# Weight chunks loaded early into idle buffers, and some counts moved to ScalarE, in a top-k attention and SoLU kernel

## The chip, the cores and the metric

The kernel runs on one core of a Trainium2 chip. The metric is the device time of one execution in microseconds (us). Engines are called by the names of the profile: PE is TensorE (PEld its weight loads), DVE is VectorE, ACT is ScalarE, POOL is GpSimd, and SP is SyncE, whose queue issues the DMAs.

## The reference

Attention that keeps, for each query, only the 32 largest scores, and behind it a feed-forward block. The weights arrive as 64-bit floats; q, k and v as 32-bit floats.

```python
# q, k, v: (8, 8, 576, 64)
scores = scale * np.matmul(q, k.transpose(0, 1, 3, 2))
kth = np.partition(scores, -32, axis=-1)[..., -32:-31]
scores = np.where(scores >= kth, scores, -1e9)
attn = np.exp(scores - max); attn = attn / (sum + 1e-9)
attn_out = np.matmul(attn, v)                 # -> x: (4608, 512)

h = x @ w_in                                  # (4608, 1024)
solu = h * softmax(h)
ln = (solu - mean) / np.sqrt(var + 1e-6) * g_ln
out = ln @ w_out                              # (4608, 512)
```

## The kernel before

Only `fast_path` runs here; a second, general path stands behind a check at the end. The attention is cut into 32 steps, four for each of the 8 batches. A step holds four chunks of 128 queries with two heads each, and a tail of 64 queries: nine score tiles of 128 x 576, numbered j = 0 to 8.

For each step `i` the work is this. `load_q`, `prep_q`, `prep_qc` bring the queries in and transpose them. `spread`, `spread_v`, `spread_r`, `first_p` and `first` estimate from the moments of the keys a first threshold `t0` for each row, near the one that 32 scores exceed; `tb` is the step by which a count moves it, and `ta` is `t0 - 31.5 tb`. `scores` multiplies, `evac` copies a tile from PSUM into `X`. `count0` counts how many scores of a row are at least `t0`, and `second` moves the threshold to `t1`; `count1` counts again, and `third` moves it to `t2`; `count2` takes signs against `t2`. `nearest`, `best` and `kth` (with `side`) find the exact 32nd value near `t2`; `exps`, `keep`, `inverse` and `norm` make the probabilities; `transpose_p`, `copy_p`, `attn_v` and `copy_v` multiply them with V.

Of the counts, all nine of `count0` and the last two of `count1` (`N1 = 2`) run on DVE (`count_v`, line 875, a comparison with the count as its sum); the first seven of `count1` run on ACT (line 897, a sign with its sum, which is twice the count less 576, with the other sign). `second` (lines 886 and 888) and `third` (lines 909, 914, 919) are tiny DVE instructions on 128 x 9 values.

The feed-forward block works on tiles of 128 tokens: `mm1`, `hexp`, `solu`, `square`, `ln`, `transpose_ln`, `copy_ln`, `mm2`, `store`.

The weights are 16 chunks of 128 x 512: 0 to 7 are `w_in`, 8 to 15 `w_out`. `load_w` brings one in (line 572) as 64-bit words. `w_bits` (DVE, lines 589, 593, 597), `w_low` (ACT, line 605), `w_mul` and `w_add` (POOL, lines 629 and 632) make a 32-bit float of it. `w_raw` has the two buffers of tag `lnT`, which the feed-forward block uses later; `w_low` has one buffer, `w_tmp` two. `w_gain` multiplies chunks of `w_out` by `g_ln`. `w_again`, `w_exp`, `w_check` read the weights once more near the end, to see that their exponents were in range.

A buffer of a pool goes round by tag: a new tile takes the next buffer of its tag, and waits until the tile that had it before is read out. Tag `X` has eight buffers (four for each step), tag `E` four.

The order of the work is written out by hand. Each call gets a time: `i * 39` plus a number from a table. `early_times` holds the tables of steps 0 to 3, `step_times` that of all later steps, `key_times`, `first_times`, `token_times`, `tails_times`, `last_times` and `weights_times` those of the rest. The calls are sorted by these times and issued in that order on every engine; the times have no other meaning. The DMAs of SP's queue stand in the same order, one behind the other.

Of the kernel before, what the change touches and what calls it, by code (L numbers as in the profile page):

```python
# [15 lines left out]
P = 128  # L16
# [427 lines left out]
def fast_path(  # L444
# [37 lines left out]
    N1 = 2  # L482
# [84 lines left out]
    def load_w(n):  # L567
        dst, src, _ = w_chunks[n]
        if w_wide:
            w_raw[n] = p2.tile([P, 512], mybir.dt.uint64, tag="lnT", name="w_raw")  # L570
            dst = w_raw[n]
        nc.sync.dma_start(out=dst, in_=src)
# [251 lines left out]
    def first(i):  # L824

        d = st[i]
        d["t0"] = small.tile([P, NT], F32, tag="t0", name="t0")
        nc.vector.tensor_tensor(out=d["t0"], in0=d["mean"], in1=d["zs"], op=ALU.add)
        d["ta"] = small.tile([P, NT], F32, tag="ta", name="ta")
        nc.vector.scalar_tensor_tensor(  # L830
            out=d["ta"], in0=d["tb"], scalar=-31.5, in1=d["t0"], op0=ALU.mult, op1=ALU.add
        )
# [47 lines left out]
    def count0(i, j):  # L880
        count_v(i, j, "t0", "c0")

    def second(i):
        d = st[i]
        u = small.tile([P, NT], F32, tag="u", name="u")
        nc.vector.tensor_tensor(out=u, in0=d["c0"], in1=d["tb"], op=ALU.mult)
        t1 = small.tile([P, NT], F32, tag="t1", name="t1")
        nc.vector.tensor_tensor(out=t1, in0=u, in1=d["ta"], op=ALU.add)  # L888
        d["t1"] = t1

    def count1(i, j):
        if j >= NT - N1:
            count_v(i, j, "t1", "n1")
            return
        d = st[i]
# [3 lines left out]
            bias=d["t1"][:, j : j + 1], accum_out=columns(i, "n1")[:, j : j + 1],  # L899
        )  # L900

    def third(i):
# [3 lines left out]
        t2 = small.tile([P, NT], F32, tag="t2", name="t2")  # L906
        groups = ((slice(0, NT - N1), -513.0, -0.25), (slice(NT - N1, NT), -31.5, 0.5))
        for js, less, _ in groups:
            nc.vector.scalar_tensor_tensor(
                out=w[:, js], in0=d["n1"][:, js], scalar=less, in1=d["tb"][:, js],  # L910
                op0=ALU.add, op1=ALU.mult,
            )
        for js, _, part in groups:
            nc.vector.scalar_tensor_tensor(
                out=t2[:, js], in0=w[:, js], scalar=part, in1=d["t1"][:, js],
                op0=ALU.mult, op1=ALU.add,
            )

# [4 lines left out]
        d["t2"] = t2  # L923
# [262 lines left out]
    def at(time, f, *args):  # L1186
        todo.append((time, len(todo), f, args))
# [40 lines left out]
            (load_q, [()], [-61.79]),  # L1228
            (prep_q, [()], [-36.38]),
            (prep_qc, [()], [-19.65]),  # L1230
            (spread, [()], [-15.66]),
            (spread_v, [()], [-15.23]),
            (spread_r, [()], [-12.41]),
            (first_p, [()], [-10.43]),
            (first, [()], [-7.18]),
            (scores, range(5), [-12.59, -9.08, -6.79, -4.4, 4.25]),
            (evac, range(9), [-10.34, -9.57, -7.99, -5.62, -0.77, -0.44, 2.85, 4.16, 4.43]),
            (count0, range(9), [2.37, -0.95, 1.47, -2.63, 10.63, 5.73, 6.8, 7.8, 12.67]),
            (count1, range(9), [19.19, 14.88, 17.69, 18.06, 19.44, 19.1, 20.48, 19.22, 17.21]),
            (count2, range(9), [31.45, 35.32, 36.51, 29.13, 28.66, 27.89, 31.39, 39.36, 37.54]),  # L1240
            (second, [()], [12.86]),
            (third, [()], [21.26]),
            (exps, range(5), [46.46, 42.79, 54.27, 60.85, 60.07]),
            (side, range(3), [38.03, 30.81, 43.23]),
            (inverse, range(3), [65.69, 70.14, 68.99]),
            (count_off, [()], [53.02]),
            (kth, [()], [58.54]),
            (nearest, range(9), [42.81, 44.99, 43.29, 31.93, 31.67, 39.85, 55.51, 55.53, 50.76]),
            (best, range(9), [43.24, 46.44, 47.92, 41.57, 35.27, 41.14, 55.57, 57, 54.82]),
            (keep, range(9), [63.82, 63.7, 64.93, 69.18, 69.36, 67.94, 66.62, 67.39, 63.89]),  # L1250
            (norm, range(9), [74.75, 67.19, 70.04, 71.03, 70.35, 76.44, 77.53, 69.09, 83.27]),
            (transpose_p, range(9), [
                77.55, 68.99, 73.92, 80.82, 73.12, 79.39, 78.11, 81.81, 84.32,
            ]),
            (copy_p, range(8), [79.4, 72.56, 77.51, 84.12, 77.59, 82.13, 81.82, 84.32]),
            (copy_pt, [()], [87.75]),
            (transpose_last, range(2), [84.59, 86.93]),
            (copy_last, range(2), [87.24, 93.94]),
            (attn_v, range(2), [89.35, 103.14]),
            (copy_v, range(2), [99.62, 103.89]),  # L1260
        ],
        [
            (load_q, [()], [-64.99]),
            (prep_q, [()], [-26.74]),
            (prep_qc, [()], [-23.56]),
            (spread, [()], [-23.23]),
            (spread_v, [()], [-20.6]),
            (spread_r, [()], [-13.67]),
            (first_p, [()], [-7.49]),
            (first, [()], [-6.58]),  # L1270
            (scores, range(5), [-21.95, -6.95, -0.08, 0.24, 5.79]),
            (evac, range(9), [-11.32, -17.27, -6.89, -6.85, 0.42, 0.09, 2.42, 4.28, 10.57]),
# [330 lines left out]
```

## Time and profile before

| | us |
|---|---|
| five runs, median | 1290.53 |
| lowest, highest | 1289.73, 1291.51 |
| the profiled execution | 1290.96 |
| its span, first to last instruction | 1289.1 |
| PE busy | 1204.0 |
| DVE busy | 1148.6 |
| ACT busy | 1119.8 |
| POOL busy | 482.1 |
| mean granted clock of PE | 0.968 |

The span is the profile's; the 1.9 us around it belong to the execution's time. Busy times are of one engine each and overlap with the others'. Where the profile says that an instruction of one line waited for another line, the text gives both. Where steps are told of, their times are read from the timeline: step 6's third threshold (line 919) comes at 263.04 us, step 8's at 333.65, step 16's at 626.37, step 31's at 1176.80.

### The profile page before, as it was taken

How to read it: one execution, taken by the hardware profiler on the slowest of the kernel's cores; microseconds unless marked ns; L12 is line 12 of the kernel's file. 1: busy time of each engine (PE TensorE's matmuls, PEld its weight loads, DVE VectorE, ACT ScalarE, POOL GpSimd, SP SyncE). 2: the span in 40 equal slices, each digit the busy share in tenths (PEclk: the TensorE clock that was granted, in tenths of full speed). 3: DMA queues.
4: the chain of work that ended last, by engine and by line, in shares of the span. 5: the costliest groups of instructions: out<-in, count | busy, mean ns of one | idle time of the engine just before them, and what ended most of it. 6: DMA issues, size and time to landing. Idle time of an engine off the chain costs nothing.

```text
span 1289.1 us, 20290 instructions
## 1 busy us (share of the span) xinstructions
PE 1204.0 (93%) x6243; PEld 657.0 (51%) x6243; DVE 1148.6 (89%) x2974; ACT 1119.8 (87%) x2446; POOL 482.1 (37%) x583
## 2 busy tenths in 40 slices
PE   7576789999999999999999999999999999998996
PEld 4243345555554555555554555555555555554443
DVE  4999999999999988999999988999999998999612
ACT  4877898999998989999999889999999889998633
POOL 4266454433442324444432334444333234443310
PEclk9567899999999999999999999999999999999998
DMA  6312111011111021011110011111110111102420
GB/s 175 96 43 70 43 43 42 18 30 38 39 36 29 19 56 38 26 31 28 47 37 26 22 48 37 35 23 36 47 37 20 29 29 36 36 1 74 133 88 28
DMA packets 106245, 56.99 MB, mean 44 GB/s; under 512 B 89224, under 2 KB 97424, under 8 KB 106128
## 3 DMA queue, kind: packets, MB, share of 16 engines
q1 hardware_dynamic: 106128, 55.61, 15.6%
q8 instruction: 52, 0.85, 0.3%
q14 instruction: 65, 0.53, 0.1%
HBM read 46.14 MB, written 9.44 MB: 43 GB/s over the span
## 4 chain that ended last, share of the span: by engine, by line
PE 51%; DVE 24%; ACT 20%; issue 4%; SPq 0%; POOL 0%; DMA 0%; DVEq 0%; ACTq 0%; POOLq 0%
PE o_ps L1170 12%; PE h_ps L1112 11%; PE s_ps L858 10%; PE tp_p L1026 6%; PE om L1083 6%; DVE junkv L875 5%; DVE E L997 5%; ACT sg L932 4%; DVE w L960 3%; DVE w L953 3%; ACT junka L897 3%; ACT PT L1038 2%; ACT E L968 2%; PE tp_ln L1159 2%; ACT X L867 2%
## 5 line engine op out<-in xcount | busy, mean ns | idle before, releaser
L1170 PE MATMUL o_ps<-w_out,lnT 128*128 128x512 f32 x576 | 261.6, 598 | 0.6 <-issue 0.6
L1012 POOL TENSOR_SCALAR E<-E,rden 128x576 f32<-128x576 f32 x256 | 205.9, 818 | 94.0 <-DVE rden L1008 85.7
L875 DVE TENSOR_SCALAR_CACHE_REDUCE junkv<-X,t 128x576 bf16<-128x576 f32 x288 | 231.0, 802 | 8.6 <-ACT X L867 4.1
L1112 PE MATMUL h_ps<-w_in,xTm 128*128 128x512 f32 x512 | 229.7, 601 | 5.3 <-ACT xTm L1098 5.3
L925 POOL TENSOR_SCALAR tt<-t 128x9 f32<-128x9 f32 x32 | 20.8, 651 | 552.8 <-DVE t L919 552.8
L953 DVE SCALAR_TENSOR_TENSOR w<-X,al,sg 128x576 f32<-128x576 f32 x256 | 212.1, 830 | 0.1
L858 PE MATMUL s_ps<-kT,qT 64*128 64x288 f32 x1024 | 201.6, 461 | 11.3 <-ACT X L867 7.9
L960 DVE MAX8 w<-w 128x8 f32<-128x576 f32 x288 | 211.4, 752 | 0.1
L997 DVE SCALAR_TENSOR_TENSOR E<-X,kth,E 128x576 f32<-128x576 f32 x256 | 199.6, 817 | 9.9 <-ACT E L968 9.6
L932 ACT ACTIVATE sg<-X,t 128x576 bf16<-128x576 f32 x256 | 196.2, 771 | 3.1 <-DVE t L919 3.0
L897 ACT ACTIVATE junka<-X,t 128x576 bf16<-128x576 f32 x224 | 174.7, 780 | 15.1 <-DVE t L888 11.5
L867 ACT ACTIVATE X<-s_ps 128x576 f32<-128x576 f32 x256 | 157.6, 654 | 33.1 <-PE s_ps L858 30.6
L1038 ACT COPY PT<-tp_p 128x512 f32<-128x512 f32 x256 | 145.7, 595 | 23.4 <-PE tp_p L1026 23.4
L1026 PE MATMUL tp_p<-ident,E 128*128 128x128 f32 x1024 | 152.6, 282 | 8.8 <-POOL E L1012 4.0
L1170 PEld LDWEIGHTS o_ps<-w_out,lnT 128*128 128x128 f32 x576 | 104.2, 190 | 110.2 <-issue 108.3
L1112 PEld LDWEIGHTS h_ps<-w_in,xTm 128*128 128x128 f32 x512 | 95.5, 192 | 117.5 <-issue 105.4
L1026 PEld LDWEIGHTS tp_p<-ident,E 128*128 128x128 f32 x1024 | 114.5, 142 | 74.3 <-issue 34.9
L1083 PE MATMUL om<-PT,vm 128*64 128x256 f32 (+1 forms) x1024 | 143.0, 423 | 5.1 <-ACT xTt L1104 5.1
L968 ACT ACTIVATE E<-X 128x1152 f32<-128x1152 f32 x128 | 147.1, 1175 | 0.6 <-PE tp_pt L1060 0.6
L858 PEld LDWEIGHTS s_ps<-kT,qT 64*128 64x128 f32 x1024 | 116.9, 200 | 58.4 <-ACT X L867 24.1
L1083 PEld LDWEIGHTS om<-PT,vm 128*64 128x64 f32 x1024 | 69.5, 140 | 65.7 <-issue 23.9
L818 POOL TENSOR_TENSOR zs<-zs,phalf 128x9 f32<-128x9 f32 x32 | 71.3, 2229 | 2.7
(127 smaller groups left out, 1627.8 us busy)
## 6 DMA issues: line engine op xcount, KB each, us to landing
km<-in_k_dram SPq DMA_DIRECT2D x32, 256.0 KB, 3.3
qm<-in_q_dram SPq DMA_DIRECT2D x128, 64.0 KB, 2.1
vm<-in_v_dram SPq DMA_DIRECT2D x32, 256.0 KB, 2.7
out_dram<-osb SPq DMA_DIRECT2D x32, 256.0 KB, 2.4
w_raw<-in_moe_w_in_dram SPq DMA_DIRECT2D x8, 512.0 KB, 4.3
w_raw<-in_moe_w_out_dram SPq DMA_DIRECT2D x8, 512.0 KB, 3.3
w_again<-in_moe_w_in_dram SPq DMA_DIRECT2D x8, 512.0 KB, 4.1
w_again<-in_moe_w_out_dram SPq DMA_DIRECT2D x8, 512.0 KB, 3.7
```

Source lines behind the costliest of these rows:

```text
L858: nc.tensor.matmul(out=s[:, half, 0:SH], lhsT=queries_of(i, t)[hd, :], rhs=kT[hd, k0 : k0 + SH], start=True, stop=True,)
L875: nc.vector.tensor_scalar(out=junk, in0=x_of(i, j), scalar1=st[i][t][:, j : j + 1], scalar2=None, op0=ALU.is_ge, op1=ALU.add, accum_out=co ...
L897: nc.scalar.activation(out=junk, in_=x_of(i, j), func=AF.Sign, scale=-1.0, bias=d["t1"][:, j : j + 1], accum_out=columns(i, "n1")[:, j : j ...
L932: nc.scalar.activation(out=d["sg", j], in_=x_of(i, j), func=AF.Sign, scale=-(1.0 + 2.0**-23), bias=d["t2"][:, j : j + 1], accum_out=column ...
L953: nc.vector.scalar_tensor_tensor(out=w, in0=x_of(i, j), scalar=d["al"][:, j : j + 1], in1=d.pop(("sg", j)), op0=ALU.subtract, op1=ALU.mult,)
L960: nc.vector.max(w8[:, j, :], st[i].pop(("w", j)))
L997: nc.vector.scalar_tensor_tensor(out=e, in0=x_of(i, j), scalar=d["kth"][:, j : j + 1], in1=e, op0=ALU.is_ge, op1=ALU.mult, accum_out=den_a ...
L1012: nc.gpsimd.tensor_scalar(out=e, in0=e, scalar1=st[i]["rden"][:, j : j + 1], scalar2=1.0, op0=ALU.mult, op1=ALU.mult,)
L1026: nc.tensor.transpose(tp[:, c, :], e[:, c * P : (c + 1) * P], ident)
L1083: nc.tensor.matmul(out=o[h * D : (h + 1) * D, cols], lhsT=vm[:, h, c, :] if c < NM else vt[hd, :], rhs=pt[:, h * NM + c, :] if c < NM else ...
L1112: nc.tensor.matmul(out=h[:, half, :], lhsT=x[:, c, :], rhs=w_in[:, c, half * 512 : (half + 1) * 512], start=(c == 0), stop=(c == NP - 1),)
L1170: nc.tensor.matmul(out=o, lhsT=d["lnT"][:, c, :], rhs=w_out[:, c, :], start=(c == 0), stop=(c == NF - 1),)
```

## The change

Three things change, and with them the tables of the order.

The raw words of chunks 2 to 5 go into buffers of tag `X`, those of chunks 6 to 9 into buffers of tag `E`; the other eight chunks stay in the two buffers of `lnT`. The loads come earlier in the order: those of chunks 2 to 9 had times from -39.22 to 56.03 and now have them from -79.38 to -7.68.

In steps 0 to 3 the last two tiles of `count0` are counted on ACT, and all nine of `count1`. From step 4 the split is as before.

`second` and `third` share a function `moved` that takes groups of columns with their own constants, one for counts of DVE and one for counts of ACT. `ta` is no longer made.

The tables `early_times`, the first batch's part of `key_times`, `first_times`, `last_times` and `weights_times` have new numbers; `step_times`, `token_times` and `tails_times` are as they were.

```diff
-    N1 = 2
+    FEW = 4
+    def n0_of(i):
+        return 2 if i < FEW else 0
+    def n1_of(i):
+        return 0 if i < FEW else 2
...
     def load_w(n):
         dst, src, _ = w_chunks[n]
         if w_wide:
-            w_raw[n] = p2.tile([P, 512], mybir.dt.uint64, tag="lnT", name="w_raw")
+            pool, tag = (p8, "X") if 2 <= n < 6 else (p4, "E") if 6 <= n < 10 else (p2, "lnT")
+            w_raw[n] = pool.tile([P, 512], mybir.dt.uint64, tag=tag, name="w_raw")
...
         nc.vector.tensor_tensor(out=d["t0"], in0=d["mean"], in1=d["zs"], op=ALU.add)
-        d["ta"] = small.tile([P, NT], F32, tag="ta", name="ta")
-        nc.vector.scalar_tensor_tensor(
-            out=d["ta"], in0=d["tb"], scalar=-31.5, in1=d["t0"], op0=ALU.mult, op1=ALU.add
-        )
...
-    def count0(i, j):
-        count_v(i, j, "t0", "c0")
-    def second(i):
-        d = st[i]
-        u = small.tile([P, NT], F32, tag="u", name="u")
-        nc.vector.tensor_tensor(out=u, in0=d["c0"], in1=d["tb"], op=ALU.mult)
-        t1 = small.tile([P, NT], F32, tag="t1", name="t1")
-        nc.vector.tensor_tensor(out=t1, in0=u, in1=d["ta"], op=ALU.add)
-        d["t1"] = t1
-    def count1(i, j):
-        if j >= NT - N1:
-            count_v(i, j, "t1", "n1")
-            return
-        d = st[i]
+    def count_a(i, j, t, c):
         junk = p1.tile([P, S], BF16, tag="junka", name="junka")
         nc.scalar.activation(
             out=junk, in_=x_of(i, j), func=AF.Sign, scale=-1.0,
-            bias=d["t1"][:, j : j + 1], accum_out=columns(i, "n1")[:, j : j + 1],
+            bias=st[i][t][:, j : j + 1], accum_out=columns(i, c)[:, j : j + 1],
         )
+    def count0(i, j):
+        (count_a if j >= NT - n0_of(i) else count_v)(i, j, "t0", "c0")
+    def count1(i, j):
+        (count_v if j >= NT - n1_of(i) else count_a)(i, j, "t1", "n1")
+    def moved(i, c, old, new, groups):
+        d = st[i]
+        w = small.tile([P, NT], F32, tag="step", name="step")
+        t = small.tile([P, NT], F32, tag=new, name=new)
+        groups = [g for g in groups if g[0].stop > g[0].start]
+        for js, less, _ in groups:
+            nc.vector.scalar_tensor_tensor(
+                out=w[:, js], in0=d[c][:, js], scalar=less, in1=d["tb"][:, js],
+                op0=ALU.add, op1=ALU.mult,
+            )
+        for js, _, part in groups:
+            nc.vector.scalar_tensor_tensor(
+                out=t[:, js], in0=w[:, js], scalar=part, in1=d[old][:, js],
+                op0=ALU.mult, op1=ALU.add,
+            )
+        d[new] = t
+    def second(i):
+        n = NT - n0_of(i)
+        moved(i, "c0", "t0", "t1", [(slice(0, n), -31.5, 1.0), (slice(n, NT), -513.0, -0.5)])
+    def third(i):
+        n = NT - n1_of(i)
+        moved(i, "n1", "t1", "t2", [(slice(0, n), -513.0, -0.25), (slice(n, NT), -31.5, 0.5)])
...
     early_times = [
...
-            (count0, range(9), [2.37, -0.95, 1.47, -2.63, 10.63, 5.73, 6.8, 7.8, 12.67]),
-            (count1, range(9), [19.19, 14.88, 17.69, 18.06, 19.44, 19.1, 20.48, 19.22, 17.21]),
+            (count0, range(9), [1.43, -2.43, -1.53, -1.4, 2.24, 3.27, 7.16, 8.56, 8.7]),
+            (count1, range(9), [19.93, 27.62, 15.8, 24.5, 16.48, 14.52, 25.06, 25.75, 22.05]),
...
-            (second, [()], [12.86]),
-            (third, [()], [21.26]),
+            (second, [()], [10.83]),
+            (third, [()], [28.34]),
...
     key_times = [
-        (load_k, [-166.62, -49.24, -48.06, -20.27], [-71.77, -54.35, -34.54, -26.23]),
+        (load_k, [-186.91, -84.21, -66.88, -51.07], [-71.77, -54.35, -34.54, -26.23]),
...
     weights_times = [
         (load_w, True, range(NW), [
-            -265.85, -158.41, -39.22, -37.42, -11.7, -5.54, -1.79, 41.13, 56.03, 50.88, 56.83,
-            71.11, 110.63, 112.61, 120.51, 116.47,
+            -264.91, -138.71, -79.38, -78.33, -63.45, -50.94, -40.81, -7.68, -10.19, -32.43,
+            2.31, 72.75, 82.5, 98.38, 126.93, 102.43,
         ]),
         (w_bits, w_wide, range(NW), [
-            -211.44, -62.88, -11.38, -5.56, 13.3, 20.41, 25.67, 80.76, 89.01, 87.79, 95.75,
-            108.28, 119.86, 122.13, 125.83, 125.77,
+            -206.1, -133.32, -59.29, -11, -8.45, -1, 8.57, 16.59, 19.71, 22, 82.33, 110.45,
+            112.29, 122.01, 131.06, 127.49,
         ]),
         (w_low, w_wide, range(NW), [
-            -194.07, -90.93, -5.49, 2.15, 11.06, 37.53, 50.76, 75.15, 83.03, 89.95, 90.55,
-            114.78, 116.95, 122.82, 127.55, 133.41,
+            -253.87, -103.51, -22.7, -12.05, -1.93, 6.53, 13.63, 20.05, 32.16, 36.18, 71.11,
+            99.32, 115.63, 118.83, 128.43, 136.12,
         ]),
...
```

## The prediction

> **What bounds the kernel now.** I read three views in this order: the 40 slices of the page, busy time by stage, and the waits of each engine inside those stages.
>
> ```profile
> PE   7576789999999999999999999999999999998996
> DVE  4999999999999988999999988999999998999612
> ACT  4877898999998989999999889999999889998633
> PEclk9567899999999999999999999999999999999998
> ```
>
> Each digit is a slice of 32.2 us. VectorE (DVE) is at nine tenths from the second slice. TensorE (PE) reaches that only in the seventh, at a granted clock of 0.5 to 0.9 until then; ScalarE (ACT) has eights and a seven early. So DVE sets the pace of the first 200 us.
>
> ```profile
> 22.70:75.00 52.30, 32.54 (x120) 17.35 (x119) 47.29 (x126) 42.99 (x96) 19.21 (x17) 0.63 0.34 97
> 75.00:120.00 45.00, 30.45 (x161) 17.95 (x159) 43.99 (x105) 32.68 (x70) 27.38 (x27) 0.77 0.22 62
> 120.00:165.00 45.00, 35.35 (x176) 18.63 (x175) 43.15 (x104) 36.54 (x81) 26.29 (x23) 0.84 0.17 49
> 165.00:205.00 40.00, 35.88 (x198) 18.98 (x197) 38.02 (x99) 36.05 (x83) 21.15 (x28) 1.00 0.16 40
> 205.00:252.00 47.00, 45.46 (x257) 25.75 (x257) 45.60 (x115) 41.54 (x87) 18.08 (x22) 1.00 0.11 30
> 521.29:556.32 35.03, 34.79 (x190) 18.98 (x188) 34.26 (x91) 33.15 (x70) 13.59 (x16) 1.00 0.06 17
> ```
>
> The columns are the stretch, its length, busy us of PE, PEld, DVE, ACT and POOL, the clock, the DMA share and GB/s. The last row is one step in the middle: 35.03 us long, DVE 98% busy. Between 75 and 120 us DVE is at that same 98%, while PE has 68% and ACT 73%. From 22.7 to 252 us ACT is busy 42.99+32.68+36.54+36.05+41.54 = 189.8 of 229.3 us, so 39.5 us are free.
>
> ```profile
> DVE junkv L875 <- ACT X L867: 2.1, 2, 1.2
> DVE step L909 <- ACT junka L897: 1.4, 1, 1.4
> DVE al L941 <- ACT sg L932: 0.6, 1, 0.6
> ```
>
> These are DVE's waits from 22.7 to 75 us (total, times, longest). From 521 to 696 us, five whole steps, it has no named wait at all, and the steps are 35.02 us apart: there too DVE is never kept waiting, with PE only about 0.4 us a step behind it (103.88 busy of 105.11 us over three steps). What shortens DVE's stream before some 230 us should therefore move everything behind it, and PE has the room early: it is idle 45-35.35 + 40-35.88 + 47-45.46 = 15.3 us from 120 to 252, and far more before.
>
> **The counts.** In steps 0 to 3, two counts of `count0` and two of `count1` go from line 875 (DVE) to the form of line 897 (ACT): sixteen in all.
>
> ```profile
> L875 DVE TENSOR_SCALAR_CACHE_REDUCE junkv<-X,t 128x576 bf16<-128x576 f32 x288 | 231.0, 802 | 8.6 <-ACT X L867 4.1
> L897 ACT ACTIVATE junka<-X,t 128x576 bf16<-128x576 f32 x224 | 174.7, 780 | 15.1 <-DVE t L888 11.5
> ```
>
> On DVE one count takes 802 ns and a read of its sum 82 ns, partly overlapped. In the timeline the next instruction starts 0.73 us after a count that stands among others (572.97 to 573.70) and 0.94 us after one in a row (569.41 to 570.35). So sixteen are worth 11.7 to 15.0 us; I take 0.81 each, 13.0 us, since the orders of the early steps mix them. On ACT the start-to-start is 0.76 (signs into different tiles, 41.27 to 42.03) to 0.90 us (counts in a row into one `junka`, 35.08 to 35.98): 12.2 to 14.4 us more, 13.3 taken. They are hidden in ACT's 39.5 free us; without that cover they would cost all 13.3. ACT then has 203 us in some 215, 94%; the middle step shows 33.15 of 35.03, 95%. It fits on the sum, but tightly.
>
> One rule of the Trainium skill speaks against this move: "Trainium Architecture — The Big Picture", section "The five engines, in one table", warns ScalarE off simple arithmetic, on which VectorE is said to be up to about 3x faster per element. By it an estimate would be 16 x 2.4 = 39 us on ACT, all that is free, and the gain would vanish. Rows of this kernel have 780 ns against 802 for the same 128x576 tile, so I go by the rows.
>
> **The loads.** Chunks 2 to 9 go to the buffers of X and E, which are free until step 1's evacuations and step 0's exponentials. Eight SP-queue issues are moved ahead, none added: 16 loads before and after. Before, each waited for one of two buffers; the queue's waits in the first 200 us hold 25.9 us for `w_low` and 23.7 us for `w_tmp`. DVE itself waited only 8.5 us for these data, all before its first count at 22.69 us; up to there it is busy 3.58+4.95 = 8.5 us, so 14.2 us lie idle. The new order puts the bits of five chunks before that count, not four, and ten before step 0's third thresholds where six stood. One chunk's bits cost 0.42+0.69+0.43 = 1.5 us of DVE. What moves into idle time is at least nothing and at most four chunks, 6.2 us; I take 2.5, one chunk before the counts and 1 us in the gaps of the evacuations (2.1 us above). In the queue, the K of pairs 2 and 3 and the Q of step 1 now stand behind 2 to 6 loads of 512 KB. At the 204 GB/s moved from 14.8 to 22.7 us each takes 2.6 us: up to 15 us later for the last of them. Before, step 1's Q was issued at 15.7 and used at 32.1 us: 16 us of cover, just enough. Without it step 1 starts late by the difference, with chunks' bits for DVE to do meanwhile.
>
> **The thresholds.** `ta` (line 830) goes from every step. In step 14 the first count starts 0.08 us after `ta` does, so 0.08 us is the saving, up to the 0.2 us of such an instruction with its gap. It counts in steps that DVE paces, some 21 of the 28 later ones (six of each eight are 35.02 us apart, the other two 40 to 42 with DVE waiting): 1.7 us, at most 4.2, at least nothing. `second` stays at two tiny instructions from step 4, four in steps 0 to 3, where `third` loses two: no net.
>
> **The new waits.** `second` in the first four steps now waits for ACT's two counts, and `third` for nine instead of seven. Queued behind each on DVE are `w` and MAX8 of the step before and the bits of weights, and for them wait ACT's next signs and POOL. The nearest row is the 1.4 us above; eight gates give 0 to 11.2 us. I take 0.6 each, 4.8, since other work is put before most of them.
>
> **The end.** The last tokens' order is changed, but from 1227 us PE runs matmuls back to back to 1278; the checks of weights on DVE and ACT lie under it. I take nothing, plus or minus 1 us.
>
> **Sum**, against the profiled execution's own 1290.96 us (span 1289.1): -13.0 -2.5 -1.7 +4.8 = -12.4, so 1278.6; the median of the runs is 0.43 lower, so 1278. With every term at its end: 15.0+6.2+4.2 = 25.4 off, 1265, or 11.7-11.2 = 0.5 off, 1290.
>
> A second place for the skill is the clock. The granted clock is 0.50 from 39 to 78 us, and eight score matmuls take 2.83 us at 25 us against 1.24 at 571 us. "TensorE: Matmul & The Clock Gate", section "Part 1: The HAM clock gate", says the clock is halved by default and released after about 3.4 us of sustained work. By the rule, a denser start would come to full clock sooner and some of PE's 22.35 busy us there would halve; by the row nothing is sure, as the clock stays low at a 57% share, and my sum has nothing for it.
>
> **The rivals.**
> - *ACT becomes the bound.* For it: 94% on the sum, in a stretch where its work comes in bursts. Then the gates cost their full 11.2 and the chunks bring nothing: -13.0-1.7+11.2 = -3.5, 1287. Against it: 39.5 us free, most of it exactly where DVE is fullest (75 to 120).
> - *PE can't follow.* For it: 97% from 205 us on, and 99% in the middle. If its order in steps 0 to 3 holds it to today's pace, only the thin early gain is left: 1289 to 1291. Against it: 15.3 idle us from 120, more before.
> - *ScalarE is blocked by the weights' chain* (the slower side). `w_low` has one buffer, so ACT can't start a chunk before POOL's two instructions on the one before. Today two of them stand 3.41 us apart (22.54 and 25.95), 0.67 of it ACT's own. If eight chunks in a row make ACT wait 2.74 us each, that is 21.9 us, plus half of the counts (6.5), less the 9.3 us that ACT has free from 22.7 to 75: 19.1 late, against 13.0+2.5+1.7 = 17.2 gained: 1293. It decides from some 20 us of such waits in that stretch; ACT has 11.5 now in 200 us. Against it: chunks 2 to 9 are placed over a longer time than that chain needs.
> - *The loads change nothing*, because DVE's order holds the conversion back and not the data: without the 2.5, 1280.6, inside my own range.
>
> **Chances.** Forecast (with the last rival) 0.60, its own range 1271 to 1284; ACT bound 0.16; PE 0.09; blocked 0.15. A measurement of this kernel tells 0.2%, 2.6 us, from no change, so the first two are faster: 0.76, same 0.09, slower 0.15. The range for eight in ten runs from 1271, inside the far end of 1265, to 1291, which takes in the second and third cases.
>
> **What would show it.** Sixteen counts fewer on line 875's successor and as many more signs on ACT, at the same 0.8 us; DVE still near 97% from 23 to 250 us, and ACT up from 83% to about 94%; step 6's `t` after its third threshold, now at 263.04 us, near 252; steps from there 34.9 to 35.0 apart; the last ones as now. DVE waiting for `junka` by more than 10 us before 200, or ACT for POOL's `w_in` by over 20, would make me wrong; so would an unchanged time of step 6.

## The result, and the profile after

The changed kernel takes 1290.53 us (median of 27 runs, 1286.63 to 1292.09), the kernel before, on the same chip, 1290.54 (49 runs): a ratio of 0.9998, with a 95% interval from 0.9992 to 1.0003. No change, where 1278 was forecast. In a later comparison the same two gave 1287.88 and 1290.31, 0.9983 [0.9974, 0.9992]. Two comparisons of one pair thus differ by 0.15%, and their intervals only touch; the change is worth between nothing and 2.4 us. The profiled execution of the changed kernel took 1287.91 us, 2.6 below its median, with a span of 1286.1; spans below are compared with spans (before: 1289.1).

The 40 slices of the changed kernel, in the order PE, DVE, ACT, clock:

```profile
PE   6567889999999999999999999999999999998996
DVE  5999899999998979999999989999999988999512
ACT  4998897999998989999998989999999889998534
PEclk9577799999999999999999999999999999999998
```

ACT now has nines in the second and third slice, where it had an eight and a seven; DVE, all nines from the second to the fourteenth slice before, has eights in the fifth and the thirteenth, and a seven in the fifteenth, where an eight stood. The same five stages (length, then busy us of PE, PEld, DVE, ACT, POOL, the clock, the DMA share, GB/s):

```profile
22.70:75.00 52.30, 30.52 (x133) 17.06 (x129) 48.79 (x113) 48.88 (x111) 25.14 (x25) 0.62 0.37 110
75.00:120.00 45.00, 36.32 (x196) 21.31 (x196) 41.75 (x102) 41.39 (x94) 26.73 (x28) 0.76 0.17 45
120.00:165.00 45.00, 35.81 (x185) 20.50 (x182) 41.15 (x99) 40.66 (x95) 27.47 (x29) 0.81 0.15 43
165.00:205.00 40.00, 35.97 (x189) 19.14 (x187) 38.99 (x94) 32.30 (x72) 13.62 (x18) 0.96 0.13 31
205.00:252.00 47.00, 44.93 (x251) 24.30 (x251) 43.91 (x111) 44.33 (x94) 12.99 (x16) 1.00 0.11 31
```

ACT, fourth of the busy columns, is at 48.88 + 41.39 + 40.66 + 32.30 + 44.33 = 207.6 of 229.3 us, 91%, up from 83%. DVE is down to 41.75 and 41.15 in the second and third stage (93% and 91%): it is no longer the one engine that is always at work. The granted clock did not come up sooner: 0.62, 0.76, 0.81 and 0.96 in the first four stages, for 0.63, 0.77, 0.84 and 1.00 before. The page's groups of the two kinds of count:

```profile
L881 DVE TENSOR_SCALAR_CACHE_REDUCE junkv<-X,t 128x576 bf16<-128x576 f32 x280 | 224.8, 803 | 15.3 <-ACT X L873 7.1
...
L889 ACT ACTIVATE junka<-X,t 128x576 bf16<-128x576 f32 x232 | 180.4, 778 | 12.6 <-DVE t L912 8.8
```

280 where 288 stood on DVE, 232 where 224 stood on ACT: eight of the sixteen. The other eight are of the tail's tile `Xt`, which the page keeps in groups of its own. Up to step 6's third threshold DVE has 61 counts of both forms where it had 77.

DVE's waits in the first 280 us:

```profile
DVE w_tmp L600 <- DMA w_raw<-in_moe_w_in_dram: 11.7, 3, 4.7
DVE junkv L881 <- ACT X L873: 3.2, 2, 2.3
DVE al L950 <- ACT sg L941: 2.7, 2, 2.3
DVE junkv L881 <- ACT Xt L873: 1.5, 1, 1.5
...
DVE step L907 <- ACT junka L889: 0.3, 1, 0.3
```

Waits for `junka`, which the sum feared most, are 0.3 us. In their place stand waits for a score tile (3.2 and 1.5, before 2.3 and 0.7), for ACT's signs (2.7, before 0.6), and 11.7 for weights where 8.5 stood before. All of the 11.7 lies ahead of the first count, and a wait of 4.3 us for `y_ps` (line 798) that stood there before is gone. So the first count, behind the bits of five chunks and no longer four, comes only 0.1 us later (before, then after):

```profile
22.69 0.81 DVE L875 TENSOR_SCALAR_CACHE_REDUCE junkv<-X,t 128x576 bf16<-128x576 f32 x1 [0.91 <-ACT X L867]
```

```profile
22.79 0.81 DVE L881 TENSOR_SCALAR_CACHE_REDUCE junkv<-X,t 128x576 bf16<-128x576 f32 x1
```

Where the time went is best read from one marker, the third threshold (`t`, line 919 before, 929 after): when it comes in step 4,

```profile
188.24 0.17 DVE L919 TENSOR_SCALAR t<-t 128x9 uint32<-128x9 uint32 x1
```

```profile
179.72 0.17 DVE L929 TENSOR_SCALAR t<-t 128x9 uint32<-128x9 uint32 x1
```

(before, then after) is 8.5 us earlier. The table gives this lead, all from the timelines, for ten of the runs told of here (us against before; plus is later); `ctrl` is a second trace of the changed kernel, and its distance from the first row says how far two traces of one kernel lie apart:

| | step 0 | step 4 | step 6 | step 31 | span |
|---|---|---|---|---|---|
| the change | +5.3 | -8.5 | -5.3 | -4.5 | -3.0 |
| ctrl | +4.8 | -9.0 | -5.7 | -5.2 | -3.3 |
| order_only | +16.3 | +12.4 | +15.6 | +16.9 | +18.8 |
| few0 | +8.7 | +4.6 | +7.9 | +8.2 | +10.2 |
| two_bufs | +11.9 | -2.7 | +0.6 | +1.5 | +2.8 |
| counts_old | +0.5 | +6.0 | +6.0 | +7.9 | +7.6 |
| old_both | +2.4 | +8.2 | +8.3 | +10.9 | +10.9 |
| old_tail | +6.5 | -7.6 | -4.4 | -4.0 | -4.1 |
| mended | +4.1 | -9.9 | -5.5 | -5.5 | -5.7 |
| mended_pe | +4.4 | -9.4 | -4.0 | -4.6 | -4.6 |

The first row is the whole story in four numbers: step 0 is 5.3 us late, steps 1 to 4 gain 13.8, 3.3 are lost again up to step 6, and 2.3 more after it.

### The profile page after: what moved, and what is told of

The parts are those of the page before. It is cut to its first block, busy times and chain, and to the rows that moved or that the text cites. A ratio compares the mean times of both kernels' runs of the same rounds, so it can differ in the third digit from the quotient of the medians.

```text
span 1286.1 us, 20283 instructions
## 1 busy us (share of the span) xinstructions
PE 1199.2 (93%) x6243; PEld 656.8 (51%) x6243; DVE 1140.8 (89%) x2910; ACT 1130.4 (88%) x2478; POOL 480.1 (37%) x583
## 3 DMA queue, kind: packets, MB, share of 16 engines
q1 hardware_dynamic: 106128, 55.61, 15.6%
## 4 chain that ended last, share of the span: by engine, by line
PE 57%; ACT 20%; DVE 16%; issue 3%; POOL 2%; DMA 1%; SPq 0%; DVEq 0%; ACTq 0%; POOLq 0%
PE o_ps L1179 14%; PE s_ps L864 12%; PE h_ps L1121 11%; PE tp_p L1035 7%; PE om L1092 6%; ACT junka L889 4%; DVE E L1006 4%; DVE junkv L881 3%; ACT sg L941 3%; DVE w L969 3%; ACT E L977 3%; DVE w L962 3%; ACT PT L1047 2%; PE tp_ln L1168 2%; ACT X L873 2%
## 5 line engine op out<-in xcount | busy, mean ns | idle before, releaser
L1021 POOL TENSOR_SCALAR E<-E,rden 128x576 f32<-128x576 f32 x256 | 203.0, 807 | 99.4 <-DVE rden L1017 94.3
L881 DVE TENSOR_SCALAR_CACHE_REDUCE junkv<-X,t 128x576 bf16<-128x576 f32 x280 | 224.8, 803 | 15.3 <-ACT X L873 7.1
L889 ACT ACTIVATE junka<-X,t 128x576 bf16<-128x576 f32 x232 | 180.4, 778 | 12.6 <-DVE t L912 8.8
L1035 PE MATMUL tp_p<-ident,E 128*128 128x128 f32 x1024 | 155.6, 285 | 15.5 <-POOL E L1021 8.9
L1047 ACT COPY PT<-tp_p 128x512 f32<-128x512 f32 x256 | 147.2, 598 | 22.8 <-PE tp_p L1035 22.7
```

The source lines that it names most:

```text
L881: nc.vector.tensor_scalar(out=junk, in0=x_of(i, j), scalar1=st[i][t][:, j : j + 1], scalar2=None, op0=ALU.is_ge, op1=ALU.add, accum_out=co ...
L889: nc.scalar.activation(out=junk, in_=x_of(i, j), func=AF.Sign, scale=-1.0, bias=st[i][t][:, j : j + 1], accum_out=columns(i, c)[:, j : j + 1],
L1021: nc.gpsimd.tensor_scalar(out=e, in0=e, scalar1=st[i]["rden"][:, j : j + 1], scalar2=1.0, op0=ALU.mult, op1=ALU.mult,)
L1035: nc.tensor.transpose(tp[:, c, :], e[:, c * P : (c + 1) * P], ident)
```

## The experiments

The expectations name theories by letters. *D*: DVE's stream sets the pace, and half of what the counts gave comes back as bits of weights that GpSimd slows. *P*: PE takes the gain back from some 180 us on. *A*: ACT is full in steps 0 to 3, so the counts gain nothing. *O*, which came after the first four runs: the new tables of steps 0 to 3, which the prediction had not priced, cost as much as the parts gain, and order, counts and loads only work together. The change is three things, so each was put back alone, within the new order and within the old.

**The changed kernel itself** (`ctrl`), nothing edited.

> The changed kernel itself, unaltered, for a second profile, since the first one (1287.9 us) lies under the median of its runs (1290.5). Theory D (VectorE's stream sets the pace, and about half of what the counts gave comes back as slower bits of weights beside GpSimd): step 6's third thresholds again some 5 us before those of the kernel before (258 against 263), the steps from there 0.05 us longer than before, and an end 0 to 3 us earlier. Theory P (TensorE sets the end from 180 us on): the idle time of TensorE up to 250 us is the same as before (58 us) and the end moves only with its clock, in either direction by 3 us.

Measured: 1287.88 against 1290.31, 0.9983 [0.9974, 0.9992], span 1285.8. Step 6's third threshold comes at 257.33 us, D's mark, and PE has idled 57.6 us up to 250 us (58.5 before), P's mark: this run does not tell the two apart. It is the zero of the runs that were compared together with it (few0, two_bufs, qt_late).

**The counts back on DVE**, order and loads kept:

```diff
-    FEW = 4
+    FEW = 0
```

> All counts of the first four steps back where they were (count0 and the last two of count1 on VectorE), the loads and the new order kept. Theory D: VectorE gets sixteen counts back, about 12 us, less the waits for ScalarE that go: 1297 to 1302. Theory A (ScalarE is full in steps 0 to 3, so that the counts gained nothing there): ScalarE falls from 92% to under 85% between 25 and 145 us and the time stays within 3 us of 1290.

Measured: 1302.09, 1.0096 [1.0081, 1.0112]; 14.2 us over the control. The third threshold of step 4 in this kernel:

```profile
192.86 0.17 DVE L929 TENSOR_SCALAR t<-t 128x9 uint32<-128x9 uint32 x1
```

That is 13.1 us after the 179.72 of the changed kernel; it is 13.1 at step 6, 12.7 at step 31, and the span is 13.2 longer: what DVE has to do more at the start comes out in full at the end. PE takes nothing back of these 13 us, so theory P falls as far as it puts the loss after step 4, and theory A falls with it. Whether PE would cap a gain beyond the changed kernel's, no run shows. And order and loads without the counts are 11.8 us *slower* than before.

**The loads back in two buffers**, each at the place where a buffer comes free for it:

```diff
-            pool, tag = (p8, "X") if 2 <= n < 6 else (p4, "E") if 6 <= n < 10 else (p2, "lnT")
+            pool, tag = p2, "lnT"
-            ... -79.38, -78.33, -63.45, -50.94, -40.81, -7.68, -10.19, -32.43, 2.31, 72.75,
+            ... -79.38, -78.33, -22.6, -10.9, -1.9, 6.6, 13.7, 20.1, 32.2, 72.75,
```

> The raw words of all sixteen chunks go through the two buffers of lnT again, each load placed just after the reading of the chunk two before it; counts and order of the rest as in the changed kernel. If the early loads matter, VectorE waits for w_raw at each of chunks 4 to 9, some 2 to 4 us each where nothing else stands between: 1295 to 1305. If it is VectorE's order and GpSimd that hold the conversion, and the early transfers only crowd the DMA engines: 1288 to 1292, with the first score matmuls back from 18.5 to about 15 us.

Measured: 1293.69, 1.0029 [1.0017, 1.004], 5.8 us over the control, between the two ranges that were expected. DVE's waits from 22.7 to 75 us:

```profile
DVE w_tmp L600 <- DMA w_raw<-in_moe_w_in_dram: 6.4, 1, 6.4
DVE w_tmp L600 <- DMA w_raw<-in_moe_w_out_dram: 3.4, 1, 3.4
```

The changed kernel has neither of them in that stretch: that is what the loads buy, in this order. The first of the two stands ahead of the first count, in front of the fifth chunk's bits (26.75 us): that count comes at 28.57 us here and at 22.79 in the changed kernel. The second stands ahead of step 0's third threshold.

**One transposition later**, that of the 64-row tails of pair 2's K and Q, so that its data need not be there so early:

```diff
-        (prep_t, [-76.64, -32, -22.27, 26.83], [-50.7, -40.81, -7.18, 29.61]),
+        (prep_t, [-76.64, -32, -9, 26.83], [-50.7, -40.81, -7.18, 29.61]),
```

> One thing moved in the changed kernel: the transposes of the tails of pair 2 go behind the first scores of step 0 instead of before them. In the changed kernel TensorE waits 3.4 us there for a transfer of 32 KB that took 5.7 us beside the weights. Theory D: the first scores start at about 15 instead of 18.5 us, step 0's thresholds come some 3 us earlier, and 1 to 3 us of that reach the end: 1287.5 to 1289.5. If the start is covered by the weights' bits on VectorE anyway: no difference, 1290 to 1291.

Measured: 1286.54, 0.997 [0.9961, 0.9979]; its span, 1285.6, is the control's within 0.2. The two intervals touch; not told apart. What the run does tell is why step 0 is late. In the changed kernel PE stands still 3.36 us for pair 2's queries, with step 0's first scores behind them at 18.45 us; here the scores start at 14.46 (14.70 before the change):

```profile
18.12 0.37 PE L706 MATMUL pre<-ident,qt 64*128 64x64 f32 x1 [3.36 <-DMA qt<-in_q_dram]
```

```profile
14.46 1.32 PE L864 MATMUL s_ps<-kT,qT 64*128 64x288 f32 x2
```

Yet step 0's third threshold comes at 44.42 us, 0.4 before the control's: PE's late start is not what holds it. What stands ahead of it on DVE in both are the bits of ten chunks, where the kernel before had six.

**The counts alone, in the old order**: the new functions, with all the tables and loads of the kernel before, the diff being that of the change without its tables and without the line on `pool, tag`.

> The kernel before with the counts alone: its order and its two buffers of weights, but two counts of count0 and two of count1 on ScalarE in steps 0 to 3, and thresholds by the new functions. Putting the counts back into the changed kernel cost 14.2 us. If they are worth that by themselves (theory D), and the loss comes from the new order of the first steps: 1277 to 1283, better than both kernels. If the old order can't use them, because ScalarE's counts stand behind its evacuations there and second waits (theory O, the new order belongs to the counts): 1287 to 1293.

Measured: 1298.46 against 1290.1, 1.0062 [1.0048, 1.0076], worse than either theory had it. The same sixteen counts that are worth 14.2 us in the new order *cost* 8.4 in the old one. DVE's wait from 22.7 to 75 us, and the two longest in the timeline:

```profile
DVE step L907 <- ACT junka L889: 5.7, 3, 2.9
```

```profile
31.11 0.17 DVE L907 SCALAR_TENSOR_TENSOR step<-c,tb 128x2 f32<-128x2 f32 x1 [1.95 <-ACT junka L889]
...
40.10 0.17 DVE L907 SCALAR_TENSOR_TENSOR step<-n,tb 128x9 f32<-128x9 f32 x1 [2.87 <-ACT junka L889]
```

The square brackets hold the idle time before the instruction. DVE stands still 1.95 us before it can move step 0's first threshold and 2.87 before its second, since ACT's counts come late in the old order; over the first 280 us there are 9.9 us of this, in seven waits.

**The same, with chunks 2 to 5 early in X**:

```diff
-            pool, tag = p2, "lnT"
+            pool, tag = (p8, "X") if 2 <= n < 6 else (p2, "lnT")
-            -265.85, -158.41, -39.22, -37.42, -11.7, -5.54, -1.79, ...
+            -265.85, -158.41, -39.22, -37.42, -37.41, -25, -1.79, ...
```

> As the kernel with the counts alone in the old order, and in addition chunks 2 to 5 go to buffers of X, chunks 4 and 5 loaded right behind 3. Going back to two buffers cost 5.8 us in the new order. In the old order the conversion of chunks 4 and 5 stands later, so the data are there in time without it: within 2 us of the kernel with the counts alone. If the loads are worth something there too: 2 to 5 us less.

Measured: 1299.92, 1.0073 [1.006, 1.0087], within noise of the kernel with the counts alone: in the old order the early loads of these four chunks bring nothing.

**The order alone**: the new tables, with `FEW = 0` and the two buffers of `two_bufs`; nothing moves to ACT and no buffer is borrowed.

> The new order alone: counts back on VectorE and weights through two buffers, but the tables of the changed kernel. With counts on ScalarE the old order gave +8.4 us and the new one 0 to -2.4; with counts on VectorE and early loads the new order gave +11.8; two buffers cost +5.8 in it. If order, counts and loads only work together (theory O): the new order alone is the worst of all, 1302 to 1310. If the parts add up, and the early loads are what made the kernel with counts on VectorE slow: 1294 to 1300.

Measured: 1308.01 against 1289.21, 1.0148 [1.0133, 1.0163], as theory O had it. DVE's waits from 22.7 to 75 us:

```profile
DVE w_tmp L600 <- DMA w_raw<-in_moe_w_in_dram: 6.7, 1, 6.7
DVE w_tmp L600 <- DMA w_raw<-in_moe_w_out_dram: 3.6, 1, 3.6
```

10.3 us in two waits for weights: with two buffers a chunk can't come in before the one two ahead of it is read out, and this order wants ten before step 0's third threshold, which is 16.3 us late here. (Seven load times, those of chunks 4 to 10, are the choice of this run and of `two_bufs`, so its price is the order's without early loads and no more general than that.)

These runs make a table (median less that of before, us):

| | counts on DVE | counts on ACT |
|---|---|---|
| old order, two buffers | 0 | +8.4 |
| old order, chunks 2 to 5 early | not run | +9.8 |
| new order, two buffers | +18.8 | +3.4 |
| new order, early loads | +11.8 | 0.0 and -2.4 |

No part is good or bad by itself: the counts alone cost, the order alone costs, and all three together come out even or up to 2.4 us ahead.

**The bits of weights without GpSimd's product** (`no_mul`): `w_mul` returns at once for chunks 2 to 9, so the product of their low words by the power of two is left out. It asks what DVE loses when GpSimd works beside it.

```diff
+        if 2 <= n < 10:
+            return
```

> The changed kernel without w_mul for chunks 2 to 9: the low words are added without their power of two, and GpSimd has eight instructions of 1.27 us less. VectorE's bits of weights take 31.3 us there against 27.6 before; single ones take 1.64 to 1.70 instead of 0.69 us, and 1.37 instead of 0.43, where GpSimd's w_mul or w_add runs beside them. If GpSimd holds them up (theory D): bits under 29.5 us in all, and 2 to 5 us less than the changed kernel's 1288 to 1290. If something else does: bits at 31 us and the time unchanged.

Measured: 1287.63 against 1290.1, 0.9981 [0.9972, 0.999], where the control had 0.9983. A stretch of the changed kernel's timeline (start, us, engine, line), and then two of the same instructions in this one:

```profile
31.60 1.27 POOL L640 TENSOR_TENSOR w_low<-w_low,w_tmp 128x512 f32<-128x512 f32 x1 [0.78 <-ACT w_low L616]
31.72 1.70 DVE L604 SCALAR_TENSOR_TENSOR w_tmp<-w_raw,w_tmp 128x512 uint32<-128x512 uint32 x1
32.95 1.59 POOL L643 TENSOR_TENSOR w_in<-w_tmp,w_low 128x512 f32<-128x512 f32 x1
33.45 1.37 DVE L608 TENSOR_SCALAR w_tmp<-w_tmp 128x512 uint32<-128x512 uint32 x1
```

```profile
35.52 0.43 DVE L600 TENSOR_SCALAR w_tmp<-w_raw 128x512 uint32<-128x512 uint32 x1
35.99 0.69 DVE L604 SCALAR_TENSOR_TENSOR w_tmp<-w_raw,w_tmp 128x512 uint32<-128x512 uint32 x1
```

Line 604 takes 0.69 us by itself and 1.70 beside line 640; line 608 takes 0.43 in most places and 1.37 here, beside line 643. Up to step 6's third threshold the bits' busy time falls from 31.3 to 26.9 us without the product, but that threshold comes no earlier (259.17 against 257.79): what is freed becomes waiting. DVE's longest waits up to there, but for the 11.6 us for weights, are these; in the changed kernel they are 3.2, none, 2.7 and 0.3:

```profile
DVE junkv L883 <- ACT X L875: 5.4, 5, 2.3
DVE yq L811 <- PE y_ps L793: 3.5, 1, 3.5
DVE al L952 <- ACT sg L943: 3.4, 3, 2.3
DVE step L909 <- ACT junka L891: 1.7, 4, 0.6
```

The hold is real, and taking this part of it away does not make the kernel faster: theory D's second half falls. The Trainium skill has a rule for it, "SBUF — State Buffer", section "Who interferes with whom": a VectorE instruction with two SBUF inputs, or in a two-port mode, and a GpSimd instruction that reads SBUF lock each other out until the first is done. The trace agrees: 31.60 + 1.27 = 32.87, and line 604 then ends after 0.55 us more, of the 0.69 that it takes by itself.

**`ta` back, from step 4 on** (`first` makes it, `second` multiplies and adds as before the change).

```diff
+        if i >= FEW:
+            d["ta"] = small.tile([P, NT], F32, tag="ta", name="ta")
+            nc.vector.scalar_tensor_tensor(
+                out=d["ta"], in0=d["tb"], scalar=-31.5, in1=d["t0"], op0=ALU.mult, op1=ALU.add
+            )
...
+        if i >= FEW:
+            d = st[i]
+            u = small.tile([P, NT], F32, tag="u", name="u")
+            nc.vector.tensor_tensor(out=u, in0=d["c0"], in1=d["tb"], op=ALU.mult)
+            d["t1"] = small.tile([P, NT], F32, tag="t1", name="t1")
+            nc.vector.tensor_tensor(out=d["t1"], in0=u, in1=d["ta"], op=ALU.add)
+            return
```

> The changed kernel with ta, u and the old second in steps 4 to 31. My prediction had 1.7 us as the gain of leaving ta out, so it would cost that here. By the trace the steps of the changed kernel are 0.05 us longer, not shorter: what ta saved is lost at al, which ends with GpSimd's last instruction on E in both kernels, and the new second starts 0.08 us later. By that reading: steps back at 35.02 us and 0.5 to 1.5 us less in all.

Measured: 1287.99 against 1290.1, 0.9987 [0.9978, 0.9996], span 1285.1. An instruction on DVE more in each of 28 steps, and the kernel is not slower. From step 6 to step 31 the trace has 913.4 us with `ta` back, 914.5 without it, 913.8 before the change. Why the removal saves nothing is in the timeline of the changed kernel's step 14:

```profile
567.13 0.74 POOL L1021 TENSOR_SCALAR Et<-Et,rden 128x576 f32<-128x576 f32 x1
...
567.25 0.63 DVE L950 SCALAR_TENSOR_TENSOR al<-n,tt 128x3 f32<-128x3 f32 x1
```

`al`, a tiny instruction of 0.16 us in most places, takes 0.63 and ends with GpSimd's `norm` beside it (567.13 + 0.74 = 567.87). It did the same before the change (572.48 + 0.56, GpSimd to 573.03), and with `ta` back it takes 0.55 again (566.70, GpSimd to 567.24). A DVE that comes 0.08 us sooner waits 0.08 us longer here. The views of waits show none of it, since the hold stands inside the instruction.

**The old tables of the last tokens and of the second reading of the weights**, all else as changed:

```diff
     last_times = [
-        (mm1, range(2), [66.47, 62.88]),
-        (hexp, [()], [66.5]),
...
-        (store, [()], [204.61]),
+        (mm1, range(2), [63.43, 54.45]),
+        (hexp, [()], [68.77]),
...
+        (store, [()], [193.64]),
```

and so for the three tables of `w_again`, `w_exp` and `w_check`.

> The changed kernel with the old order of the last tokens and of the second reading of the weights. From step 31's third thresholds to the end the kernel before takes 112.3 us, the changed one 114.2. If the new tables of the end cost that: 1.5 to 2.5 us less than the changed kernel, 1285.5 to 1287.5. If it is only the state in which the last steps arrive: no difference, 1288 to 1290.

Measured: 1288.72 against 1289.21, 0.9993 [0.9984, 1.0002], span 1285.0. The median alone shows no gain. The traces do. The changed kernel's last 6 us, and then this kernel's (DVE's `hit` reductions, and PE's last matmul):

```profile
1275.28 0.45 DVE L1557 TENSOR_SCALAR_CACHE_REDUCE hit<-zk_all 128x288 f32<-128x288 f32 x1 [3.39 <-ACT junka L633]
...
1277.32 0.17 DVE L1557 TENSOR_SCALAR_CACHE_REDUCE hit<-w_ok 128x16 f32<-128x16 f32 x1
...
1277.64 0.19 PE L1562 MATMUL tp_ok<-ok,ones 128*1 128x6 f32 x2 [3.73 <-DVE hit L1557]
```

```profile
1272.08 0.45 DVE L1557 TENSOR_SCALAR_CACHE_REDUCE hit<-zk_all 128x288 f32<-128x288 f32 x1 [0.88 <-ACT junka L633]
...
1275.46 0.17 DVE L1557 TENSOR_SCALAR_CACHE_REDUCE hit<-w_ok 128x16 f32<-128x16 f32 x1 [1.46 <-ACT junka L633]
...
1275.78 0.19 PE L1562 MATMUL tp_ok<-ok,ones 128*1 128x6 f32 x2 [1.69 <-DVE hit L1557]
```

In the changed kernel a check of weights on ACT, the last but one, holds DVE for 3.39 us, all the reductions of `hit` then run in a row, and PE's last matmul waits 3.73. With the old tables the long reductions are done while ACT still copies the last output, and PE waits 1.69. The 3.7 is in the traces of all eight kernels with the new end, the 1.7 in all five with the old one and in the kernel before. From step 31's third threshold to PE's last matmul it is 105.4 us in all eight, and 103.0 with the old end (103.8 in `mended_pe`). What follows that matmul takes 7.3 to 9.4 us and is on the whole shorter with the new end, so not all of the 2.4 us reach the end of the span: from step 31's third threshold to there it is 113.8 and 114.2 us in the changed kernel's two traces, 112.3 before and 112.2 here. This kernel also comes to that threshold 0.5 and 1.2 us later than those two traces.

**What the runs suggest, together** (`mended`): pair 2's transposition later, `ta` back, the old end.

> Three things mended in the changed kernel: the transposes of pair 2's tails behind the first scores (1.3 us less by itself), the old first, ta and second from step 4 on (0 to 0.7 us), the old tables of the end (1.9 us by the trace). If they add up: 1283 to 1286.5. If one pace behind them swallows them (TensorE, theory P): 1286.5 to 1289.

Measured: 1284.22 against 1289.21, 0.9953 [0.9941, 0.9965], span 1283.4: 5.0 us faster than before, and its interval lies below both of the changed kernel's (0.9992 to 1.0003 and 0.9974 to 0.9992). Most of what is won over the changed kernel is the end: at step 31 `mended` is 5.5 us ahead of before, the changed kernel 4.5 and 5.2 in its two traces, and from there to PE's last matmul it takes 103.0 us for 105.4.

**And the 3.3 us between steps 4 and 6** (`mended_pe`). In every kernel with the new order, whatever the counts and loads, at least 3.2 us are lost there against before (4.4 in `mended`); in those with the old order next to nothing (the table above). In `mended` PE waits there for GpSimd's probabilities:

```profile
PE tp_p L1047 <- POOL E L1033: 3.3, 1, 3.3
```

so two of step 3's transpositions were put later, behind other matmuls:

```diff
-            (transpose_p, range(9), [69.88, 69.41, 75.48, ...
+            (transpose_p, range(9), [70.9, 70.5, 75.48, ...
```

> The same, and in step 3's table the first two groups of transposes of probabilities go behind the first scores of step 5. All kernels with the new order lose 3.3 us between the third thresholds of steps 4 and 6 against the kernel before; there TensorE waits 3.3 us for GpSimd's E, and VectorE then 1.5 us for the tail's scores. If that wait is the cause: 1 to 3 us less than the kernel with three things mended, and step 4 to 5 at 40 to 41 instead of 42.4 us. If it is work of VectorE that was only put off to here: no difference.

Measured: 1285.15, 0.9962 [0.995, 0.9974], not faster than `mended`. The wait is gone, and another has its place:

```profile
PE s_ps L869 <- DVE rs L1149: 2.8, 1, 2.8
```

DVE's own wait of 1.5 us for the tile `Xt` stays, and 5.4 us are lost between the two thresholds, not 4.4. Part of the 3.3 is no loss: two MAX8, some 1.4 us, that stood ahead of step 4's threshold before stand behind it in the new order. And the traces show one thing more. In the changed kernel, too, PE waits 3.3 us for `E`, up to 187.60 us, and in the 8 us behind that wait its granted clock is low. These 8 us before the change (there the wait is 1.8 us long), in the changed kernel, in `mended` and in `mended_pe`; the clock is the third number from the right:

```profile
193.85:201.85 8.00, 7.42 (x32) 3.95 (x34) 7.68 (x21) 6.17 (x17) 5.37 (x6) 1.00 0.21 47
187.60:195.60 8.00, 8.00 (x28) 4.11 (x30) 7.90 (x21) 5.08 (x13) 3.76 (x5) 0.79 0.18 39
186.19:194.19 8.00, 8.00 (x23) 4.62 (x24) 7.90 (x21) 4.99 (x13) 3.76 (x5) 0.62 0.19 41
186.13:194.13 8.00, 7.41 (x17) 3.85 (x18) 7.90 (x20) 4.01 (x12) 3.85 (x5) 0.58 0.20 44
```

From the one threshold to the other PE is busy 70.9, 72.7, 73.8 and 74.7 us in the four, and DVE stands idle 2.5, 4.1, 5.1 and 6.3. The other eight traces with the new order show the same 0.79 there. So a slower PE behind the wait is a rival to the wait itself, and it fits that `mended_pe`, which only put another wait there, lost more. No run tests it: this stays open.

## Why the prediction was wrong

**The failed step** is in the loads: "The new order puts the bits of five chunks before that count, not four, and ten before step 0's third thresholds where six stood", and then "What moves into idle time is at least nothing". Bits that are put ahead could only gain by it; what they hold up was given no price, here or elsewhere in the sum. Of the two halves the first came true: the fifth chunk did go into idle time, for the first count comes at 22.79 us, and at 22.59 in `few0`, where it came at 22.69. The second did not. From the first count to step 0's third threshold pass 26.1 us in `few0`, with the same counts on DVE as before, where 17.4 passed. The bits of weights in this stretch (stretch, its length, busy us of DVE and POOL, the clock, the DMA share, GB/s; before, then `few0`):

```profile
22.69:40.05 17.36, 3.17 (x6) 7.61 (x6) 0.88 0.55 162
22.59:48.70 26.11, 11.34 (x15) 12.80 (x10) 0.80 0.60 177
```

Five chunks stand there for two, and with GpSimd beside them they take 11.3 us, where five at 1.5 would take 7.7. These 8.2 us more are most of the 8.7 that step 0 is late. Four counts off DVE take 3.2 of them away (4 x 0.81), and the changed kernel is 5.3 late. What was done ahead does not all come back: from step 0's threshold to step 4's DVE has 9.0 us less to do in `few0` than before (134.0 for 143.0), but it stands idle some 5 us more, so the order gives back only half (+4.6), loses 3.3 up to step 6 and 2.0 at the end. Up to step 6's third threshold the account of DVE, third of the busy columns, is this (before, `few0`, the changed kernel):

```profile
0.00:263.04 263.04, 204.34 (x1025) 112.39 (x1025) 237.43 (x594) 209.37 (x460) 121.06 (x140) 0.86 0.24 65
0.00:270.91 270.91, 195.64 (x1025) 110.44 (x1025) 241.35 (x586) 209.11 (x460) 115.52 (x140) 0.84 0.23 63
0.00:257.79 257.79, 199.61 (x1025) 111.78 (x1025) 230.67 (x555) 221.05 (x492) 117.63 (x140) 0.84 0.24 66
```

Order and loads give DVE 3.9 us more of work and 4.0 more of idle time; the sixteen counts then take 10.7 us of work and 2.4 of idle time away. So the bound should have been below nothing, and the new tables needed a term of their own: 11.8 us with early loads, 18.8 without them, where the sum had +0.6 for all but the counts (-2.5 -1.7 +4.8). That the order costs this is shown by the runs. How it falls on the chunks ahead of step 0's threshold is an account of busy time only, since no run put these chunks back alone; and in `no_mul`, where they take 8.9 us there for 12.7, that threshold is no earlier (46.42 us for 45.35), so that PE's and ACT's work in that stretch has a part in it too.

**The second fault** is that the terms were added at all. They depend on each other: counts +8.4 in one order and -14.2 in the other, early loads +1.5 (no more than noise) and -5.8.

Term by term, within the new order:
- *Counts, -13.0*: right in size. The change is ahead of `few0` by 13.1 us at step 4, by 14.2 in the median.
- *New waits, +4.8, up to 11.2*: 9.9 us in the old order, 0.3 in the new one. "since other work is put before most of them" was the right reason; the new tables are that cover, and their price is the order's.
- *Loads, -2.5*: -5.8 against the new order with two buffers, near the end of 6.2 given, but not by the reason given: they take away 9.8 us of waits (6.4 ahead of the first count and 3.4 behind it, in `two_bufs`) that the kernel before did not have and that the new order makes.
- *`ta`, -1.7*: nothing. "DVE is never kept waiting" was read from a view that cannot show a hold inside an instruction. The busy time beside it was misread as well: the three steps hold 103.53 us of PE, not 103.88, and 102.81 of DVE, so that PE is no less full there than DVE.
- *The end, 0 plus or minus 1*: +2.4 up to PE's last matmul, 1.5 and 1.9 in the spans of the changed kernel's two traces. "the checks of weights on DVE and ACT lie under it" holds for the old tables, not for the new ones.

**The rivals.** By the time alone, PE's case (1289 to 1291) is met by the first comparison, 1290.53, and ACT's (1287) is near the second, 1287.88; that is luck in both. ACT's mark, DVE waiting for `junka`, is 0.3 us; ACT is at 91%, and DVE's waits for score tiles and signs, 7.4 us in the first 280 where 3.6 stood, are what is true of it. For PE speaks that it has idled 58.2 us at 252 us and 58.7 before; but there is an early gain of 13 us from `few0` to the changed kernel, and it is found at the end in full: of that, PE held nothing back. ScalarE blocked by the weights: one wait of 3.7 us for line 643, not eight of 2.74. Loads that change nothing: refuted in the new order, true in the old. Of the marks that were set, ACT's rise came near (91% for 94%) and step 6's threshold did not: 257.79 us for 252, before 263.04. DVE's "still near 97%" was off from the start: by the rows shown it is busy 218.1 of 229.3 us before, 95%, and 214.6 after, 94%. None of the three signs of being wrong came, since none of them looked at the order.

## What to carry to other kernels

A hand-made order and the engine that each piece of work runs on are one design: a diff with new tables in it needs a price for the tables, from what is now put behind what, and its parts cannot be summed from prices that hold in the old order. Before a tiny instruction on a full engine is counted as time, look in the timeline whether a neighbour is being held, for a hold inside an instruction counts as busy. And the end of a kernel deserves its own look: here 2.4 us hung on which of two small chains came last.

## What was not expected of the hardware

DVE's instructions of 0.69, 0.43 and 0.16 us took 1.70, 1.37 and 0.63 when GpSimd's ran beside them, without a wait in any view. A transfer of 32 KB of queries, issued at 12.38 us, took 5.71 in the chain of waits, with three loads of 512 KB issued from 10.05 to 14.31; the median of its kind in the first 30 us is 3.1. PE's granted clock was 0.79 in the 8 us behind a wait of 3.3 us (0.62 in `mended`), and 1.00 behind one of 1.8 us before the change. And the changed kernel's median stood 2.6 us apart in two comparisons (1290.53 and 1287.88) while the kernel before kept 1290.5 and 1290.3: for a gain as small as this one both kernels are needed in several comparisons.
